# First MoE of a three-stage kernel: gate and value products with the weights as the stationary operand, no transposes of the gated rows

## The chip, the cores and the metric

The kernel runs on one core of a Trainium2 chip. A core has a matrix engine (PE, with its weight loads shown apart as PEld), three elementwise engines (DVE, ACT, POOL), and DMA queues, of which SP issues most here. Each engine works through its own list of instructions in order. The metric is device time in microseconds (us), the median of several executions. The profile is one execution.

## The reference

Three stages follow one another: attention in which every row keeps its 32 largest scores, a gated feed-forward block ("first MoE", one expert), and a routed block of eight experts.

```python
x = topk_attention(q, k, v)                 # 1152 tokens x 512 (8 heads of 64), top 32 of 576 scores
xn = x / rms(x) * rms_g
g = xn @ w_gate                             # 512 -> 1536
silu = g * (1.0 / (1.0 + np.exp(-g)))
val = xn @ w_val                            # 512 -> 1536
y = silu * val @ w_out                      # 1536 -> 512
out = routed_experts(y)                     # 8 experts, each 512 -> 1024 -> 512, one per token
```

The change concerns only `g`, `val` and the way in which `silu * val` reaches the product with `w_out`.

## The kernel before

The 1152 tokens are nine tiles of 128. Attention runs over 36 pairs of heads (nine tiles, four pairs each): scores on PE (L317, tile `tp`), a copy by ACT (L319), the top 32 by DVE (L324 to L379), masking and exponentials by ACT and POOL (L398, L399, L404), nine transposes of the weights by PE (L422, copied by ACT at L423), and the product with the values by PE (L430, tile `xps`).

The first MoE of a tile begins when its four pairs are done. `norm` scales the rows and leaves `xn`, the turned rows (512 channels on partitions, 128 tokens), as a high and a low float16 half. `moe1(t, ew)` then goes over three groups g of 512 hidden channels. For each it computes the gate product and the value product (b = 2g and 2g + 1). A product is 12 matmuls: four chunks c of 128 channels, each with three combinations of high and low halves. `xn` is the stationary operand (a load of 128 x 128) and 512 columns of the weights (`half(i, lo)`, in `wbig`) stream through, so the result `a` in PSUM (tile `pm`, three buffers; `late` for some of the last tile) has tokens on partitions. That is 72 matmuls a tile at L502 and 648 in all.

The gate is activated and multiplied with the value product into `h` (tile `gs`, one buffer; `x` once in the last tile). Tiles 0, 7 and 8 use ACT and DVE for this (L510, L511, L514), tiles 1 to 6 ACT and POOL (L516 to L523, with `gs` also holding the scaled gate, written at L517). The product with `w_out` (L531, 36 matmuls a tile, 128 x 512) needs `h` with the hidden channels on partitions. `turned(g, h)` does that: four 128 x 128 transposes on PE (L486) into a `pm` tile, then `halves`: ACT copies it to the high half of `hT` (L470), DVE subtracts to get the low half (L471). It is called in the middle of the gate product of the next group, and for the last group among the matmuls of L531.

The order on each engine is made by a scheduler from priorities: attention has a head start of 200 to 400 in `ahead`, `moe1` has none, so first-MoE work fills in behind attention and falls behind it. For the last tile (t = 8) the order on PE is fixed by `after(...)`: the products of group g + 1 wait behind the transposes of group g. After the last pair ("the tail") PE has the rest of tiles 6, 7 and 8, while ACT and DVE prepare the first expert weights: squares (L795), high halves (L820, L822), low halves (L825). The routed stage starts at L920 when tile 8 is through.

Of the kernel before, what the change touches and what calls it, by code (L numbers as in the profile page):

```python
# [8 lines left out]
F32 = mybir.dt.float32  # L9
# [53 lines left out]
def whole(  # L63
# [415 lines left out]
    def moe1(t, ew):  # L479
        hT = [mx.tile([P, 2 * KC, P], F16, name="hT", bufs=3) for _ in range(3)]  # L480
        xn = xnT.pop(t)

        def turned(g, h):
            tp = pm.tile([P, 4, P], F32, name="pm")
            for i in range(4):
                behind[t, "turn", g] = nc.tensor.transpose(tp[:, i, :], h[:, i * P:(i + 1) * P], ident)  # L486
            behind[t, "dve"] = halves(hT[g], tp)

        h = None
        for g in range(3):  # L490
            th = mx.tile([P, DM], F32, name="th")
            if ew is nc.gpsimd:
                gs = mx.tile([P, DM], F32, name="gs")
            for w in range(2):
                b = 2 * g + w
                ahead_of = (None, ("prod", 0), None, ("turn", 0), None, ("turn", 1))[b] if t == NT - 1 else None
                a = late[0].tile([P, DM], F32, name="late") if late and b % 3 else pm.tile([P, DM], F32, name="pm")
                for c in range(KC):
                    i = KC * b + c
                    with after(t, *ahead_of) if ahead_of else nullcontext():  # L500
                        for n, (x, lo) in enumerate(((0, 0), (0, 1), (KC, 0))):
                            behind[t, "prod", b] = nc.tensor.matmul(  # L502
                                a, xn[:, x + c, :], half(i, lo), start=(c == 0 and n == 0), stop=(c == KC - 1 and n == 2))
                    if c == 1:
                        yield
                    if c == 0 and w == 0 and h is not None:
                        turned(g - 1, h)
                yield
                if w == 0 and ew is nc.vector:
                    behind[t, "tanh", g] = nc.scalar.activation(th, a, AF.Tanh, scale=gdec[:, g:g + 1])  # L510
                    behind[t, "th", g] = nc.vector.scalar_tensor_tensor(th, th, 1.0, a, op0=OP.add, op1=OP.mult)  # L511
                elif ew is nc.vector:
                    h = mx.tile([P, DM], F32, name="x" if t == NT - 1 and g == 1 else "gs")
                    behind[t, "gs", g] = nc.vector.scalar_tensor_tensor(h, a, vg[:, g:g + 1], th, op0=OP.mult, op1=OP.mult)  # L514
                elif w == 0:
                    nc.scalar.activation(th, a, AF.Tanh, scale=gdec[:, g:g + 1])  # L516
                    nc.scalar.activation(gs, a, AF.Copy, scale=gdec[:, g:g + 1])  # L517
                    ew.tensor_tensor(th, th, gs, op=OP.mult)
                    ew.tensor_tensor(th, th, gs, op=OP.add)
                else:  # L520
                    h = mx.tile([P, DM], F32, name="gs")
                    nc.scalar.activation(h, a, AF.Copy, scale=vdec[:, g:g + 1])
                    ew.tensor_tensor(h, th, h, op=OP.mult)  # L523
        yps = pm.tile([P, DM], F32, name="pm")
        for f in range(NF1):
            i = final(6, f)
            if f == (2 if t == NT - 1 else 4):
                turned(2, h)
            with after(t, *(("prod", 5) if f < 2 else ("turn", 2))) if t == NT - 1 else nullcontext():
                for n, (hi, lo) in enumerate(((0, 0), (0, 1), (1, 0))):  # L530
                    nc.tensor.matmul(yps, hT[f // KC][:, KC * hi + f % KC, :], half(i, lo), start=(f == 0 and n == 0), stop=(f == NF1 - 1 and n == 2))  # L531
            if f % 2 == 1:
# [598 lines left out]
```

## Time and profile before

| what | value |
|---|---|
| median of three runs | 655.77 us (653.97 to 659.06) |
| the profiled execution | 654.35 us, its span 652.4 us |
| granted TensorE clock, mean | 0.984 |
| PE busy | 583.8 us, 89% of the span |
| DVE, ACT, POOL busy | 533.5, 501.6, 355.6 us (82%, 77%, 55%) |
| share of the chain that ended last | PE 61%, DMA 10%, DVE 9%, ACT 8%, POOL 6% |

The span has four parts: loading and weight conversion up to about 147 us, attention together with the first MoE up to 459 us (the last L430), the tail up to 514.4 us (the last transposes of tile 8 before the first L920), and the routed experts to the end. A row of a timeline merges equal instructions that follow one another: its first number is the start, its second the time to the end of the last of them, and x12 says how many. The pace of a run of matmuls is therefore read from ends: the end of one row (start plus duration) minus the end of the row before it, divided by the count. The duration of a single matmul is longer than its pace, because matmuls overlap.

### The profile page before, as it was taken

The numbers are of one execution on the slowest core, as the hardware profiler recorded it, in microseconds if no ns is written. First come the engines' busy times: TensorE is split into PE (matmuls) and PEld (weight loads), VectorE is DVE, ScalarE is ACT, GpSimd is POOL, SyncE is SP. The second block draws the span as 40 slices with busy tenths as digits, with TensorE's granted clock in tenths as the row PEclk, the third lists the DMA queues.
The fourth block names the chain that finished last, engine by engine and source line by source line (L and its number), as shares of the span: only waits on it lengthen the run. The fifth ranks groups of instructions, "written<-read, shape, count | busy, mean of one in ns | idle before, by whom it ended". The sixth has DMA issues, their size and how long they took to land.

```text
span 652.4 us, 13434 instructions
## 1 busy us (share of the span) xinstructions
PE 583.8 (89%) x4817; PEld 409.2 (63%) x4817; DVE 533.5 (82%) x1439; ACT 501.6 (77%) x972; POOL 355.6 (55%) x490
## 2 busy tenths in 40 slices
PE   1427879799999999999999999999999879999995
PEld 1314455445666666767666666565555579999994
DVE  3989999968989979998988999882359756999951
ACT  4469978997787968978887889786499538999811
POOL 2487644646358879958878789686121310123312
PEclk9999979899999999999999999999999989999998
DMA  8998345923000010100000000004900479999201
GB/s 233 296 329 292 118 175 194 311 76 78 30 13 29 14 49 10 34 18 26 18 10 34 16 13 14 2 1 179 354 16 8 156 192 390 340 321 359 97 23 43
DMA packets 47006, 80.05 MB, mean 123 GB/s; under 512 B 18716, under 2 KB 23324, under 8 KB 46930
## 3 DMA queue, kind: packets, MB, share of 16 engines
q1 hardware_dynamic: 45138, 74.28, 35.2%
q0 software_dynamic: 1792, 4.83, 1.9%
q8 instruction: 39, 0.64, 0.4%
q14 instruction: 37, 0.30, 0.1%
HBM read 64.35 MB, written 12.27 MB: 117 GB/s over the span
## 4 chain that ended last, share of the span: by engine, by line
PE 61%; DMA 10%; DVE 9%; ACT 8%; POOL 6%; issue 3%; SPq 2%; POOLq 0%; DVEq 0%; ACTq 0%
PE pm L502 16%; PE acc L920 15%; PE pm L531 9%; PE xps L430 6%; PE tp L317 5%; PE tp L422 4%; ACT junk L795 3%; DMA disp<-wraw 2%; DMA wbig<-in_k_l_dram 2%; DVE r L373 2%; PE pm L486 2%; POOL pp L399 1%; DVE wbig L168 1%; DMA raw<-in_w_dram 1%; DVE wbig L169 1%
## 5 line engine op out<-in xcount | busy, mean ns | idle before, releaser
L502 PE MATMUL pm<-wbig,xn 128*128 128x512 f16 x600 | 145.4, 379 | 0.5 <-DVE hT L471 0.5
L920 PEld LDWEIGHTS <-split 128*128 128x128 f16 x1728 | 114.8, 99 | 5.1 <-DMA xbT<-xb 3.2
L399 POOL TENSOR_TENSOR pp<-s,pp 128x576 f32<-128x576 f32 x72 | 102.1, 1434 | 23.1 <-ACT pp L398 22.9
L502 PEld LDWEIGHTS <-xn 128*128 128x128 f16 x648 | 62.6, 98 | 60.6 <-issue 0.9
L376 DVE MAX8 m<-r 128x8 f32<-128x288 f32 x216 | 96.7, 452 | 2.5
L373 DVE MATCH_REPLACE8 r<-m,r 128x288 f32<-128x288 f32 x216 | 95.2, 443 | 0.0
L317 PE MATMUL tp<-kst,qh 128*128 128x288 f32 (+1 forms) x160 | 64.4, 410 | 32.8 <-ACT s L319 14.9
L531 PE MATMUL pm<-wbig,hT 128*128 128x512 f16 x324 | 76.7, 380 | 0.0
L825 DVE SCALAR_TENSOR_TENSOR split<-raw,sc,split 128x2048 f16<-128x2048 f32 (+1 forms) x32 | 65.9, 2076 | 0.1
L319 ACT ACTIVATE s<-tp 128x288 f32<-128x288 f32 x144 | 57.3, 421 | 10.5 <-PE tp L317 8.8
L423 ACT ACTIVATE pt<-tp 128x384 f32<-128x384 f32 x108 | 52.2, 503 | 15.3 <-PE tp L422 10.8
L317 PEld LDWEIGHTS tp<-kst,qh 128*128 128x128 f32 (+1 forms) x160 | 31.1, 195 | 51.1 <-ACT s L319 21.1
L430 PE MATMUL xps<-pt,vt 128*64 128x128 f32 (+1 forms) x800 | 62.4, 275 | 0.0
L422 PE MATMUL tp<-ident,pp 128*128 128x128 f32 x324 | 57.9, 288 | 4.9 <-DVE r L325 2.6
L398 ACT ACTIVATE pp<-s,bias 128x576 f32<-128x576 f32 x72 | 52.3, 779 | 9.4 <-POOL bias L381 9.3
L920 PE MATMUL acc<-hE,split 128*128 128x168 f16 (+2 forms) x864 | 58.9, 228 | 0.3 <-DVE hE L932 0.3
L404 ACT ACTIVATE pp<-pp,bias 128x576 f32<-128x576 f32 x72 | 57.1, 795 | 2.3 <-POOL pp L399 2.1
L920 PE MATMUL acc<-xgT,split 128*128 128x168 f16 (+1 forms) x768 | 56.4, 234 | 0.4 <-issue 0.4
L795 ACT ACTIVATE junk<-raw 128x2048 bf16<-128x2048 f32 (+1 forms) x32 | 54.1, 1689 | 3.2 <-DMA raw<-in_w_dram 2.9
L422 PEld LDWEIGHTS tp<-ident,pp 128*128 128x128 f32 x324 | 40.2, 145 | 23.7 <-DVE r L325 3.4
L430 PEld LDWEIGHTS xps<-pt,vt 128*64 128x64 f32 x800 | 43.9, 138 | 13.7 <-issue 12.0
L531 PEld LDWEIGHTS <-hT 128*128 128x128 f16 x324 | 29.8, 98 | 32.0 <-issue 1.0
(237 smaller groups left out, 1225.5 us busy)
## 6 DMA issues: line engine op xcount, KB each, us to landing
raw<-in_w_dram SPq DMA_DIRECT2D x28, 1024.0 KB, 9.4
wbig<-in_w_gate_dram SPq DMA_DIRECT2D x6, 1024.0 KB, 7.7
wbig<-in_w_val_dram SPq DMA_DIRECT2D x6, 1024.0 KB, 9.1
wraw<-in_w_out_dram SPq DMA_DIRECT2D x12, 512.0 KB, 5.9
disp<-wraw SPq DMA_DIRECT2D x18, 257.0 KB, 6.4
qraw<-in_q_l_dram SPq DMA_DIRECT2D x72, 64.0 KB, 2.2
wbig<-in_k_l_dram SPq DMA_DIRECT2D x16, 288.0 KB, 4.0
split<-in_w_dram SPq DMA_DIRECT2D x4, 1024.0 KB, 8.3
```

The costliest lines, as they stand in the source:

```text
L317: nc.tensor.matmul(sp[:c1], x[:, i, :c1], kst[b, hp][:, i, c * HALF:(c + 1) * HALF], start=(n == 0), stop=(n == 1))
L319: nc.scalar.activation(s[:, c * HALF:(c + 1) * HALF], sp, AF.Copy)
L373: nc.vector.match_replace(h[i], to[n - 1][:, i], h[i], -3.0e38)
L376: nc.vector.max(to[n][:, i], h[i])
L399: nc.gpsimd.tensor_tensor(w, s[i], w, op=OP.subtract)
L422: nc.tensor.transpose(tp[:, i, :], p2[:, o:o + P], ident)
L430: nc.tensor.matmul(xps[t][rows, hp, c0:c1], v, w, start=(n == 0), stop=(n == 4))
L502: behind[t, "prod", b] = nc.tensor.matmul(a, xn[:, x + c, :], half(i, lo), start=(c == 0 and n == 0), stop=(c == KC - 1 and n == 2))
L531: nc.tensor.matmul(yps, hT[f // KC][:, KC * hi + f % KC, :], half(i, lo), start=(f == 0 and n == 0), stop=(f == NF1 - 1 and n == 2))
L795: nc.scalar.activation(junk, raw[:, g * 2 * BIG // k:(g + 1) * 2 * BIG // k], AF.Square, accum_out=sc[:, 3 + g:4 + g])
L825: nc.vector.scalar_tensor_tensor(lo[:, r], raw[:, r], sc[:, 1:2], hi[:, r], op0=OP.mult, op1=OP.subtract)
L920: nc.tensor.matmul(a, u[:, c, col * P:(col + 1) * P], v[:, c, :a.shape[-1]], start=(c == 0 and n == 0), stop=(c == nk - 1 and n == 2))
```

## The change

Both products are computed turned: 128 columns of the weights are the stationary operand and the 128 tokens of `xn` stream through. A result `a` has the same size and the same place, but now has hidden channels on partitions, as four blocks j of 128 channels, each accumulated over 12 matmuls. A product is thus 48 matmuls of 128 x 128, each with a weight load of its own; a tile has 288 and all nine have 2592. `h` comes out as L531 needs it, so the transposes go, and `halves` reads `h` in SBUF directly (`activated`). The two orders by `after` in the last tile are adapted. What activates and multiplies is unchanged. (In the changed file the product is L499, the product with `w_out` L529, the gate copies L514 and L515.)

```diff
-        def turned(g, h):
-            tp = pm.tile([P, 4, P], F32, name="pm")
-            for i in range(4):
-                behind[t, "turn", g] = nc.tensor.transpose(tp[:, i, :], h[:, i * P:(i + 1) * P], ident)
-            behind[t, "dve"] = halves(hT[g], tp)
+        def activated(g, h):
+            behind[t, "dve"] = halves(hT[g], h.rearrange("p (j w) -> p j w", j=KC))
...
-                ahead_of = (None, ("prod", 0), None, ("turn", 0), None, ("turn", 1))[b] if t == NT - 1 else None
+                ahead_of = ("prod", b - 1) if t == NT - 1 and b else None
...
-                for c in range(KC):
-                    i = KC * b + c
+                for j in range(KC):
                     with after(t, *ahead_of) if ahead_of else nullcontext():
-                        for n, (x, lo) in enumerate(((0, 0), (0, 1), (KC, 0))):
-                            behind[t, "prod", b] = nc.tensor.matmul(
-                                a, xn[:, x + c, :], half(i, lo), start=(c == 0 and n == 0), stop=(c == KC - 1 and n == 2))
-                    if c == 1:
+                        for c in range(KC):
+                            for n, (x, lo) in enumerate(((0, 0), (0, 1), (KC, 0))):
+                                behind[t, "prod", b] = nc.tensor.matmul(
+                                    a[:, j * P:(j + 1) * P], half(KC * b + c, lo)[:, j * P:(j + 1) * P], xn[:, x + c, :],
+                                    start=(c == 0 and n == 0), stop=(c == KC - 1 and n == 2))
+                    if j == 1:
                         yield
-                    if c == 0 and w == 0 and h is not None:
-                        turned(g - 1, h)
+                    if j == 0 and w == 0 and h is not None:
+                        activated(g - 1, h)
...
-                turned(2, h)
-            with after(t, *(("prod", 5) if f < 2 else ("turn", 2))) if t == NT - 1 else nullcontext():
+                activated(2, h)
+            with after(t, "prod", 5) if t == NT - 1 else nullcontext():
```

The scheduler orders the instructions anew, on every engine. Three places are shown, first as they stood and then as they stand.

On PE, in the middle of attention: before, the transposes of `h` (L486, written to `pm`) stand between the matmuls of the product (L502, `xn` loaded).

```order
L447 MATMUL px<-ident,xu 128x128 x4
L486 MATMUL pm<-ident,gs 128x128 x2
L502 LDWEIGHTS xn
L502 MATMUL pm<-wbig,xn 128x512
L502 LDWEIGHTS xn
L502 MATMUL pm<-wbig,xn 128x512
L486 MATMUL pm<-ident,gs 128x128
L502 LDWEIGHTS xn
L502 MATMUL pm<-wbig,xn 128x512
L486 MATMUL pm<-ident,gs 128x128
```

On PE at a like place after: the product is L499, with `wbig` loaded and `xn` streaming, and it stands behind the transposes of the attention weights (L422).

```order
L529 LDWEIGHTS hT
L529 MATMUL pm<-wbig,hT 128x512
L422 MATMUL tp<-ident,pp 128x128 x3
L499 LDWEIGHTS wbig
L499 MATMUL pm<-xn,wbig 128x128
L499 LDWEIGHTS wbig
L499 MATMUL pm<-xn,wbig 128x128
```

The transposes of `h` are gone from the product; where one load of `xn` stood before a matmul of 512 columns, four loads of `wbig` stand before four matmuls of 128.

On PE, at the end of the tail: before, matmuls of L531 on `hT` of tile 8, then the small matmuls of the routing of tile 7 (L598, L599), then the transposes of the last `h` (L486), then the 30 remaining matmuls of L531.

```order
L531 MATMUL pm<-wbig,hT 128x512
L805 LDWEIGHTS ones_70
L805 MATMUL st<-sc,ones_70 128x1
L598 LDWEIGHTS before
L598 MATMUL px<-oh,before 128x8
L599 LDWEIGHTS ones_70
L599 MATMUL px<-cum,ones_70 128x8
L486 MATMUL pm<-ident,gs 128x128 x4
L531 LDWEIGHTS hT
L531 MATMUL pm<-wbig,hT 128x512
```

The same place on PE after (L529 is the product with `w_out`, L596 and L597 are the routing of tile 7).

```order
L529 LDWEIGHTS hT
L529 MATMUL pm<-wbig,hT 128x512
L596 LDWEIGHTS before
L596 MATMUL px<-oh,before 128x8
L597 LDWEIGHTS ones_70
L597 MATMUL px<-cum,ones_70 128x8
L529 LDWEIGHTS hT
L529 MATMUL pm<-wbig,hT 128x512
```

The 36 matmuls of this product (now L529) run on, with only the routing matmuls between them (now L596, L597); nothing on PE stands between them that reads `h` itself.

On ACT, in the middle of attention (the name in brackets is the engine whose counter is waited for): before, the copy of the scaled gate into `gs` (L517) waits for PE, whose transposes were the last readers of the buffer, and the copy `hT` (L470) comes behind it.

```order
L398 ACTIVATE pp<-s,bias 128x576
L423 ACTIVATE pt<-tp 128x384 [waits PE_49,Activation_49]
L517 ACTIVATE gs<-pm,st 128x512 [waits PE_49]
L470 ACTIVATE hT<-pm 128x512
L423 ACTIVATE pt<-tp 128x384 [waits PE_49]
```

On ACT at a like place after (L514 is the tanh of the gate, L584 belongs to the routing).

```order
L470 ACTIVATE hT<-gs 128x512 [waits Pool_49]
L584 ACTIVATE ex,nm<-lg,nm 128x8 [waits Pool_49]
L514 ACTIVATE th<-pm,st 128x512 [waits PE_49]
L515 ACTIVATE gs<-pm,st 128x512 [waits DVE_49]
L398 ACTIVATE pp<-s,bias 128x576 [waits Pool_49]
```

Now `hT` (L470) is copied from `gs` itself, and the next gate copy into `gs` (L515) waits for DVE, whose subtraction (L471) is now the last reader of the one buffer. All 18 gate copies of tiles 1 to 6 wait for DVE in this way.

## Rows read from the trace of the kernel before

**Rows 1.** Windows: attention with first MoE, the tail, its ACT-heavy part

```profile
core 0: us, PE busy (x) PEld busy (x) DVE busy (x) ACT busy (x) POOL busy (x), PEclk, DMA share, GB/s
147.00:459.00 312.00, 310.26 (x2173) 199.72 (x2171) 268.35 (x886) 253.97 (x568) 234.12 (x323) 1.00 0.10 33
459.00:514.40 55.40, 53.68 (x293) 28.39 (x293) 36.53 (x75) 41.73 (x75) 12.52 (x26) 1.00 0.34 122
475.00:507.00 32.00, 31.06 (x179) 16.56 (x178) 26.32 (x54) 30.71 (x55) 5.68 (x11) 1.00 0.08 28
```

**Rows 2.** Longest waits of PE from 147 to 507 us (total, times, longest)

```profile
PE pm L486 <- DVE nm L604: 0.6, 1, 0.6
```

**Rows 3.** Groups by line (busy us, mean ns): weight loads of full arrays

```profile
L920 PEld LDWEIGHTS <-split 128*128 128x128 f16 x1728 | 114.8, 99 | 5.1 <-DMA xbT<-xb 3.2 <-issue 1.5
```

**Rows 4.** Timeline of PE: transposes of h, and 512-column matmuls

```profile
454.12 0.59 PE L531 MATMUL pm<-wbig,hT 128*128 128x512 f16 x2
454.56 0.60 PE L486 MATMUL pm<-ident,gs 128*128 128x128 f32 x4
...
506.46 0.66 PE L486 MATMUL pm<-ident,gs 128*128 128x128 f32 x4 [0.64 <-DVE nm L604]
506.95 6.64 PE L531 MATMUL pm<-wbig,hT 128*128 128x512 f16 x30
```

**Rows 5.** Timeline of PE: float16 matmuls with a new weight load each

```profile
518.54 4.18 PE L920 MATMUL acc<-xgT,split 128*128 128x128 f16 x72
...
524.28 4.79 PE L920 MATMUL acc<-hE,split 128*128 128x128 f16 x83 [0.29 <-DVE hE L932]
532.06 3.84 PE L920 MATMUL acc<-xbT,split 128*128 128x48 f16 x96 [2.98 <-DMA xbT<-xb]
535.74 0.64 PE L961 MATMUL back<-ident,yT 128*128 128x128 f32 x4
```

**Rows 6.** Timeline of PE: borders between kinds of matmul

```profile
74.75 1.08 PE L193 MATMUL tp<-wbig 128*128 128x128 bf16 x16
75.64 0.38 PE L317 MATMUL tp<-kst,qh 128*128 128x288 f32 x1
...
308.23 0.88 PE L430 MATMUL xps<-pt,vt 128*64 128x128 f32 x12
309.03 0.87 PE L422 MATMUL tp<-ident,pp 128*128 128x128 f32 x6
...
337.41 1.25 PE L502 MATMUL pm<-wbig,xn 128*128 128x512 f16 x5
338.31 0.49 PE L317 MATMUL tp<-kst,qh 128*128 128x288 f32 x1
...
338.86 0.88 PE L430 MATMUL xps<-pt,vt 128*64 128x128 f32 x12
339.66 0.40 PE L317 MATMUL tp<-kst,qh 128*128 128x288 f32 x1
```

**Rows 7.** Timeline of ACT and DVE: hT copies and the subtractions behind them

```profile
250.43 0.61 ACT L470 ACTIVATE hT<-pm 128x512 f16<-128x512 f32 x1
...
253.11 0.68 DVE L471 TENSOR_TENSOR hT<-pm,hT 128x512 f16<-128x512 f32 x1
...
353.85 0.60 ACT L470 ACTIVATE hT<-pm 128x512 f16<-128x512 f32 x1
...
355.09 0.67 DVE L471 TENSOR_TENSOR hT<-pm,hT 128x512 f16<-128x512 f32 x1
```

**Rows 8.** Timelines of PE and ACT: marks of the tail

```profile
457.68 1.31 PE L430 MATMUL xps<-pt,vt 128*64 128x128 f32 x20
...
466.06 0.27 PE L544 MATMUL px<-ident,yx 128*128 128x128 f32 x1
...
472.95 0.63 ACT L455 ACTIVATE x<-xu 128x512 f32<-128x512 f32 x1 [0.20 <-DVE xu L452]
...
508.86 0.57 ACT L470 ACTIVATE hT<-pm 128x512 f16<-128x512 f32 x1
```

## The prediction

> **What bounds the kernel now.** I read the windows by stage first, then the waits of PE, then the timeline of PE row by row. The products that change run from 147 us to the end of the tail at 514.4 us. In the attention stretch PE is busy 310.3 of 312 us, in the tail 53.7 of 55.4; DVE has 268.4 of the 312, ACT 254.0, POOL 234.1, and the granted clock is 1.00 throughout [rows 1], which is the 2.4 GHz level. Busy time of PE alone proves little, since matmuls overlap, so the waits count: the longest of PE in these 360 us is 0.64 us [rows 2], and the ends of the rows in its timeline follow one another at a fixed pace. So PE sets the end of both stretches; what its list loses in time the kernel gains, until DVE (86% of the attention stretch) or ACT takes its place. In the tail ACT is the second: 30.7 of 32 us busy from 475 to 507 [rows 1], from the square of tile 8 (ACT L455, 472.95 us) to its last hT copy (508.86 us) [rows 8]. The routed stage hangs on the end of tile 8 and should move with it.
>
> **The change part by part.**
>
> *Transposes removed.* Four of them stand in one row: its end is 455.16, that of the row before 454.71, so 0.45 us for four [rows 4]. 27 groups of four go: 27 x 0.45 = 12.1 us less on PE.
>
> *Products.* Thirty matmuls of 512 columns end 6.47 us after the row before them (513.59 less 507.12), so 0.2157 us each [rows 4]; 648 of them are 139.8 us. For 128 columns with a load each, two runs of L920 are of the very form that the change uses (float16, full array, a new load for each, 12 matmuls into the same 128 columns of PSUM in the first): 72 take 4.18 us and 83 take 4.79, so 11 more take 0.61, 0.0555 us each [rows 5]. 2592 x 0.0555 = 143.9 us: 4.1 us more. A load lasts 99 ns by itself [rows 3], but a pace of 0.0555 shows that it runs under the matmuls before it; with 48 columns, 96 pairs take 3.84 us, 0.040 each [rows 5], so at 128 columns the load is not yet what limits. The upper bound of the pace is 4.18 / 72 = 0.0581, or 10.8 us more.
>
> *Borders.* A 512-column matmul hides the load of whatever follows; one of 128 hides less. A score matmul (L317) ends 0.14 us after a 512-column row, 0.19 after the 128-column rows of L193 (bf16, a load each) [rows 6]: 0.05 us more. Four float32 transposes behind L920 need 0.48 instead of 0.45 [rows 5, 4]: 0.03 more. By the order of PE, products now stand directly before scores 64 times and before float32 transposes and their like 86 times: 3.2 + 2.6 = 5.8 us. Against that, products now separate work that stood together: L430 before scores 10 times instead of 21, where the border is 0.32 instead of 0.14, and before L422 17 times instead of 31, where six transposes need 0.79 instead of 0.675 [rows 6]: 11 x 0.18 + 14 x 0.115 = 3.6 us less. Net 2.2 us more. Bounds: nothing at the new borders (5.8 less than taken), or what a border behind L430 costs at all of them (64 x 0.18 + 86 x 0.115 = 21.4, or 15.6 more). I take the values behind L193 and L920, which use the full array as the new matmuls do; L430 uses 64 columns of it.
>
> *The gap at the end.* Before the last transposes PE stands idle for 0.64 us, waiting for DVE [rows 4]. After, 24 matmuls of the last product (24 x 0.2157 = 5.2 us) cover the making of the last hT: 0.6 us less.
>
> PE in sum: -12.1 + 4.1 + 2.2 - 0.6 = -6.4 us. It does not fall evenly. The new order leaves 576 small matmuls and 96 of L529 behind the last L430, where 132 and 84 and 24 transposes stood: 52.7 us instead of 49.3. So the tail is 3.4 - 0.6 = 2.8 us longer, and the attention stretch some 9.2 us shorter. The work that ACT does in the tail begins earlier with it.
>
> *What is moved and waits.* ACT now copies hT from `gs`, which saves the way through PSUM but keeps the one `gs` buffer until DVE has subtracted; the next gate copy (18 of them) stands on ACT behind that, and behind it the score copies and exponentials that DVE and PE want. DVE ended its subtraction 2.75 us after the ACT copy in one place (253.79 less 251.04) and 1.31 in another (355.76 less 354.45) [rows 7]. In the new order of ACT, 9 of the 18 have only 0.7 to 2.5 us of other work between copy and gate copy, 14.8 us together by the mean durations; the others have more than 2.75. So ACT waits 1.5 us in all at a lag of 1.31 and 9 x 2.75 - 14.8 = 10 us at 2.75. ACT has 58 us free in this stretch [rows 1], so most of it is absorbed: I take 2 us, between 0 and 10. SP and the DMAs change in nothing but their start; the `pm` buffers have three tiles fewer to hold per tile of tokens.
>
> Total: -6.4 + 2 = -4.4 us, 649.95 against the profiled execution's 654.35. The median of the runs, 655.77, lies 1.4 above that execution, so on the median's scale 651.4; I predict 651.
>
> **The rivals.** *The load is not hidden* (slower by far). If each load of 99 ns [rows 3] set the pace, 2592 would take 256.6 us: 116.8 more, less 12.1, about 759. Rows 5 speak against it at the same form. The Trainium skill (TensorE: Matmul & The Clock Gate, "The mechanism" under packing small matmuls) states that a weight load overlaps with matmuls in flight only when it is for other rows of the array; and its section "Back-to-back issue gap" gives a sustained 81 ns per matmul at 128 columns and 131 at 512, by which the products alone would cost 210 - 85 = 125 us more. The trace disagrees with both here: full-array loads run under full-array matmuls, and the paces are 55.5 and 215.7 ns. Chance 0.02.
>
> *Another engine takes the slack* (no change). If DVE, ACT and POOL need the 312 us whatever PE does, only the tail moves: 654.35 + 2.8 = 657, or 658.5 on the median's scale; with half of the 9.2 us kept, 654. For it: DVE would have to work at 268 of 303 us, 89%, with ACT at 84%, and the three feed one another for each pair of heads. Against it: PE hardly waits for them now. Chance 0.22 for 654 to 659.
>
> *ACT waits for DVE at `gs` and PE feels it* (slower). The place is the gate copy of tiles 1 to 6. With the whole 10 us on the path the sum is -6.4 + 10 = +3.6, some 659; if all 18 copies lose 2.75 us it is 49.5 - 6.4, near 699. It decides where the 18 cost over 6.4 us of PE's time, 0.36 us each. For it: such a wait holds up all that stands behind it on ACT. Against it: half of the 18 have room. Chance 0.13, mostly 658 to 668.
>
> *No loss anywhere.* Borders cost nothing and ACT absorbs everything: -12.1 + 4.1 - 3.6 - 0.6 = -12.2, 642 (643.5 on the median's scale). Chance 0.13 for 641 to 646.5.
>
> **How the numbers follow.** The forecast, 646.5 to 654, has 0.50. About 1%, 6.5 us, is what a measurement of this kernel can tell from no change: below 649.2 is faster, above 662.3 slower. Below 649.2 lie the last rival and a bit under half of the forecast: 0.13 + 0.23 = 0.36. Above 662.3 lie the unhidden load and most of the wait at `gs`: 0.02 + 0.09 = 0.11; I give 0.14, since a new order on every engine can hold a wait that I did not see. Within 1%: 0.50. The range 643 to 661 leaves out the unhidden load, the worse part of the wait at `gs` and the best of the last rival, about 2 in 10.
>
> **What would show it.** Right: L499 at 0.0555 us in runs; no L486; the last L430 near 450 us and the first L918 near 509; PE still without waits of over a microsecond; 0.19 us for a score behind L499. The wait at `gs` shows as idle time of ACT before L515 ended by DVE L471; another bound shows as PE idle before L422 or L317, ended by ACT or POOL. The prediction is wrong if L499 runs at 80 ns or more, or if the attention stretch does not shrink.

## The result and the profile after

The changed kernel takes 660.83 us (median of 9 runs, 659.37 to 663.26) beside 654.98 for the kernel before (9 runs, 653.13 to 659.06): a ratio of 1.0078, 95% interval 1.0057 to 1.0098. It is slower by 5.9 us. 651.0 was predicted, 4.8 below before; the range of 643 to 661 holds the time at its very edge, and the direction was wrong.

The profiled execution of after has a span of 658.0 us. That of before (652.4) began its first product at 146.66 us, after at 148.56. Up to there the instructions of both are the same, so I took a second profile of the unchanged kernel before (the run "before again" below): span 653.5, first product at 148.57. With equal starts the two spans differ by 4.5 us, and the windows say where. They are cut at four marks: first product, end of the last L430, end of the last matmul with `w_out`, first copy of the first expert's hidden rows (`hE`) on ACT, end. Windows of after (columns as in rows 1):

```profile
148.56:450.52 301.96, 297.84 (x3575) 246.50 (x3573) 259.62 (x884) 251.00 (x566) 235.03 (x320) 1.00 0.10 32
450.52:513.44 62.92, 59.91 (x729) 47.61 (x728) 39.23 (x75) 44.63 (x77) 17.56 (x26) 0.97 0.34 126
513.44:527.73 14.29, 7.55 (x68) 7.07 (x68) 7.46 (x28) 6.80 (x11) 4.03 (x8) 0.65 0.27 85
527.73:658.00 130.27, 119.92 (x1769) 117.85 (x1767) 96.45 (x125) 86.27 (x96) 25.02 (x17) 0.98 0.71 219
```

The same windows of the kernel before, second profile:

```profile
148.57:460.85 312.28, 310.61 (x2175) 199.92 (x2173) 268.78 (x887) 254.05 (x570) 234.19 (x324) 1.00 0.11 33
460.85:515.46 54.61, 53.67 (x293) 28.37 (x292) 35.74 (x74) 40.98 (x73) 12.55 (x26) 1.00 0.33 122
515.46:523.16 7.70, 5.91 (x66) 5.56 (x67) 6.89 (x27) 4.90 (x9) 1.17 (x3) 0.83 0.55 160
523.16:653.50 130.34, 119.57 (x1770) 118.05 (x1768) 96.98 (x127) 87.66 (x98) 28.28 (x18) 0.98 0.70 221
```

Attention is 10.3 us shorter, the tail 8.3 longer, the way from the end of the tail to the first `hE` 6.6 longer (14.29 against 7.70), the experts equal: -10.3 + 8.3 + 6.6 - 0.1 = +4.5. Beside the first profile of before, the third window is 7.4 longer (14.29 against 6.92) and the experts 1.6 shorter, +3.7 in all. In the third window PE of after is busy for half of the time, at a mean granted clock of 0.65.

**The third window.** PE of after, where rows 4 and 5 stood for before:

```profile
505.46 5.34 PE L529 MATMUL pm<-wbig,hT 128*128 128x512 f16 x24
510.64 0.17 PE L596 MATMUL px<-oh,before 128*128 128x8 bf16 x1
510.69 2.75 PE L529 MATMUL pm<-wbig,hT 128*128 128x512 f16 x12
515.11 0.63 PE L542 MATMUL px<-ident,yx 128*128 128x128 f32 x4 [1.67 <-DVE yn L563]
522.41 7.77 PE L918 MATMUL acc<-xgT,split 128*128 128x128 f16 x89 [1.63 <-DMA xgT<-disp]
```

Tile 7's routing (L596) stands behind 24 of tile 8's matmuls with `w_out`; before, it ran at 505.63, ahead of 30 of them. What hangs on it is seen on DVE, POOL and SP of after:

```profile
507.79 2.48 DVE L823 SCALAR_TENSOR_TENSOR split<-raw,sc,split 128x1024 f16<-128x1024 f32 x2
510.18 2.31 DVE L820 TENSOR_SCALAR split<-raw,sc 128x1024 f16<-128x1024 f32 x2
512.41 2.47 DVE L823 SCALAR_TENSOR_TENSOR split<-raw,sc,split 128x1024 f16<-128x1024 f32 x2
514.80 0.15 DVE L604 SCALAR_TENSOR_TENSOR scr<-px,oh 128x8 f32<-128x8 f32 x1
...
516.11 1.12 POOL L619 DMA_INDIRECT disp<-yd,slot  x1 [0.33 <-POOL slot L617]
...
450.60 60.05 SPq L777 DMA_DIRECT2D raw<-in_w_dram  x6
519.10 1.36 SPq L834 DMA_TRANSPOSE xgT<-disp  x1
```

The masked sum of tile 7's routing (L604) now stands behind six conversions of expert weights on DVE. So the scatter of tile 7's rows (POOL L619) starts at 516.11, the gather of the first expert's rows (SP L834) at 519.10, and the first expert's products wait for it until 522.41. PE's wait of 1.67 us for DVE (L563) ends behind the same six conversions. In the first profile of before the same steps, and PE's first products of the first expert, are:

```profile
505.63 0.17 PE L598 MATMUL px<-oh,before 128*128 128x8 bf16 x1 [0.30 <-POOL oh L595]
514.94 1.51 PE L920 MATMUL acc<-xgT,split 128*128 128x128 f16 x24
...
506.45 0.15 DVE L606 SCALAR_TENSOR_TENSOR scr<-px,oh 128x8 f32<-128x8 f32 x1
...
508.71 1.10 POOL L621 DMA_INDIRECT disp<-yd,slot  x1 [0.29 <-POOL slot L619]
...
511.66 1.36 SPq L836 DMA_TRANSPOSE xgT<-disp  x1
...
513.75 0.37 SPq L779 DMA_DIRECT2D raw<-in_w_dram  x1
```

There the gather was under way before the tail ended, and 24 products of the first expert ran at 514.94, under tile 8's dispatch. On SP the last piece of a weight load stood behind the gather (L779, 513.75); now all six pieces stand ahead of it.

**The second window.** ACT, then PE of after, between 482 and 488 us, and the windows there:

```profile
482.69 0.58 ACT L470 ACTIVATE xn<-xps 128x512 f16<-128x512 f32 x1
...
482.33 0.18 PE L803 MATMUL st<-sc,ones 128*128 128x1 bf16 x1 [0.88 <-DVE sc L806]
482.83 0.16 PE L803 MATMUL st<-sc,ones 128*128 128x1 bf16 x1 [0.32 <-ACT junk L793]
483.31 0.27 PE L499 MATMUL pm<-xn,wbig 128*128 128x128 f16 x2 [0.32 <-ACT xn L470]
484.04 4.13 PE L499 MATMUL pm<-xn,wbig 128*128 128x128 f16 x46 [0.45 <-DVE xn L471]
...
484.00:488.20 4.20, 4.16 (x50) 4.16 (x50) 4.20 (x6) 4.20 (x7) 0.00 (x0) 0.64 0.00 0
488.20:495.00 6.80, 6.80 (x114) 6.33 (x112) 6.80 (x8) 6.71 (x12) 0.00 (x0) 1.00 0.01 2
```

Before, that copy stood here:

```profile
478.36 0.59 ACT L470 ACTIVATE xn<-xps 128x512 f16<-128x512 f32 x1
```

Tile 8's copy of its normed rows on ACT (`xn`) runs at 482.69, behind ten squares of expert weights (L793); before, at 478.36 behind three. PE waits 0.88 + 0.32 us at the sums of these squares (L803), then 0.32 + 0.45 us for the copy and its low half, all in a row, and its next 46 matmuls take 4.13 us instead of the 2.6 that 46 x 0.0556 gives: the clock is 0.64 in their window, 1.00 behind it.

### The profile page after: what moved, and what is told of

Its sections match the earlier page's. It is cut to its first block, busy times and chain, and to the rows that moved or that the text cites. A ratio compares the mean times of both kernels' runs of the same rounds, so it can differ in the third digit from the quotient of the medians.

```text
span 658.0 us, 17080 instructions
## 1 busy us (share of the span) xinstructions
PE 581.0 (88%) x6653; PEld 477.7 (73%) x6653; DVE 529.6 (80%) x1439; ACT 502.3 (76%) x972; POOL 361.0 (55%) x490
## 4 chain that ended last, share of the span: by engine, by line
PE 36%; DVE 22%; POOL 13%; DMA 12%; ACT 8%; issue 5%; SPq 2%; POOLq 0%; DVEq 0%; ACTq 0%
PE acc L918 12%; PE pm L499 10%; DVE r L373 4%; PE pm L529 4%; DVE m L376 3%; DVE split L823 3%; PE xps L430 3%; DMA vt<-in_v_l_dram 3%; POOL pp L399 3%; PE tp L317 2%; DMA raw<-in_w_dram 2%; PE tp L422 2%; DVE wbig L168 2%; DMA disp<-wraw 2%; DVE wbig L169 2%
## 5 line engine op out<-in xcount | busy, mean ns | idle before, releaser
L499 PE MATMUL pm<-xn,wbig 128*128 128x128 f16 x2400 | 167.8, 220 | 2.4 <-DVE th L509 0.9
L499 PEld LDWEIGHTS <-wbig 128*128 128x128 f16 x2592 | 156.5, 99 | 17.1 <-issue 6.0
L918 PEld LDWEIGHTS <-split 128*128 128x128 f16 x1728 | 116.0, 99 | 7.9 <-issue 6.1
L376 DVE MAX8 m<-r 128x8 f32<-128x288 f32 x216 | 95.1, 450 | 1.6
L317 PE MATMUL tp<-kst,qh 128*128 128x288 f32 (+1 forms) x160 | 62.9, 399 | 34.0 <-ACT s L319 16.0
L529 PE MATMUL pm<-wbig,hT 128*128 128x512 f16 x324 | 78.2, 379 | 1.9 <-ACT hT L470 0.9
L398 ACT ACTIVATE pp<-s,bias 128x576 f32<-128x576 f32 x72 | 52.5, 783 | 14.3 <-POOL bias L381 14.2
L422 PE MATMUL tp<-ident,pp 128*128 128x128 f32 x324 | 58.0, 287 | 3.9 <-DVE r L325 2.2
L918 PE MATMUL acc<-xgT,split 128*128 128x168 f16 (+1 forms) x768 | 58.9, 240 | 2.7 <-DMA xgT<-disp 1.6
L793 ACT ACTIVATE junk<-raw 128x2048 bf16<-128x2048 f32 (+1 forms) x32 | 54.2, 1694 | 8.7 <-DMA raw<-in_w_dram 8.2
L918 PE MATMUL acc<-hE,split 128*128 128x168 f16 (+2 forms) x864 | 59.3, 228 | 0.5 <-DVE hE L930 0.5
L423 ACT ACTIVATE pt<-tp 128x384 f32<-128x384 f32 x108 | 50.1, 499 | 12.2 <-PE xps L430 6.9
L430 PE MATMUL xps<-pt,vt 128*64 128x128 f32 (+1 forms) x800 | 57.9, 273 | 0.0
L529 PEld LDWEIGHTS <-hT 128*128 128x128 f16 x324 | 29.3, 98 | 31.4 <-DVE hT L471 1.5
L430 PEld LDWEIGHTS xps<-pt,vt 128*64 128x64 f32 x800 | 43.4, 139 | 10.0 <-issue 7.8
L317 PE MATMUL tp<-kst,ql 128*128 128x288 f32 (+1 forms) x160 | 48.7, 309 | 0.0
```

The costliest lines, as they stand in the source:

```text
L317: nc.tensor.matmul(sp[:c1], x[:, i, :c1], kst[b, hp][:, i, c * HALF:(c + 1) * HALF], start=(n == 0), stop=(n == 1))
L376: nc.vector.max(to[n][:, i], h[i])
L422: nc.tensor.transpose(tp[:, i, :], p2[:, o:o + P], ident)
L430: nc.tensor.matmul(xps[t][rows, hp, c0:c1], v, w, start=(n == 0), stop=(n == 4))
L499: behind[t, "prod", b] = nc.tensor.matmul(a[:, j * P:(j + 1) * P], half(KC * b + c, lo)[:, j * P:(j + 1) * P], xn[:, x + c, :], start=(c = ...
L918: nc.tensor.matmul(a, u[:, c, col * P:(col + 1) * P], v[:, c, :a.shape[-1]], start=(c == 0 and n == 0), stop=(c == nk - 1 and n == 2))
```

## The experiments

The theories at first: (1) the new order behind attention costs, whatever the form; (2) the turned form itself costs; (3) ACT waits for DVE at `gs`; (4) work left over from attention costs behind it. The trace of after settles the third: ACT waited for DVE at L515 for 1.1 us in 3 waits, over 18 gate copies. All runs in one table; stages are cut as above, in us, of the profiled execution (of before, the first); ratios are to the kernel before, run beside each.

| run | time | ratio (95%) | first product at | attention | tail | to first hE | rest |
|---|---|---|---|---|---|---|---|
| before | 654.98 | 1 | 146.7 | 312.3 | 54.6 | 6.9 | 131.9 |
| after | 660.83 | 1.0078 (1.0057, 1.0098) | 148.6 | 302.0 | 62.9 | 14.3 | 130.3 |
| e1 | 661.24 | 1.0077 (1.0045, 1.0109) | 150.3 | 301.9 | 61.2 | 12.4 | 133.6 |
| e2 | 668.60 | 1.0210 (1.0167, 1.0252) | 148.6 | 311.1 | 60.0 | 13.0 | 133.6 |
| e3 | 664.13 | 1.0127 (1.0092, 1.0162) | 149.2 | 302.0 | 63.3 | 11.0 | 136.9 |
| e4 | 661.45 | 1.0071 (1.0047, 1.0094) | 147.8 | 302.0 | 60.8 | 11.7 | 135.7 |
| e5 | 666.93 | 1.0158 (1.0104, 1.0212) | 147.4 | 312.3 | 54.7 | 15.4 | 135.1 |
| e9 | 667.56 | 1.0181 (1.0133, 1.0229) | 146.7 | 312.2 | 54.7 | 14.2 | 135.7 |
| e6 | 665.78 | 1.0129 (1.0066, 1.0192) | 150.7 | 301.8 | 61.1 | 14.1 | 137.5 |
| e7 | 658.26 | 1.0035 (1.0009, 1.0060) | 149.2 | 301.9 | 61.1 | 13.3 | 132.3 |
| e8 | 660.70 | 1.0074 (1.0042, 1.0106) | 148.1 | 301.9 | 64.2 | 10.3 | 133.2 |
| e10 | 657.28 | 1.0022 (0.9992, 1.0052) | 149.3 | 301.9 | 62.4 | 7.5 | 132.3 |
| e11 | 654.54 | 0.9977 (0.9953, 1.0002) | 152.2 | 301.3 | 61.1 | 10.1 | 130.9 |
| e12 = before again | 655.37 (one run) | | 148.6 | 312.3 | 54.6 | 7.7 | 130.3 |
| e13 | 654.80 | 0.9970 (0.9952, 0.9989) | 146.6 | 302.0 | 60.1 | 10.7 | 130.2 |
| e14 | 654.84 | 0.9977 (0.9959, 0.9995) | 148.2 | 301.8 | 61.4 | 9.4 | 131.3 |
| e15 (old form) | 657.65 | 1.0024 (0.9997, 1.0050) | 149.8 | 312.3 | 55.0 | 6.6 | 134.5 |

### Halves of the change: e1 and e2

```diff
+        form = t < NT - 2      # e1; e2: t >= NT - 2; the old form and its transposes otherwise
```

> The turned form for tiles 0 to 6 alone; tiles 7 and 8 keep the form and the waits of before, so that the stretch behind attention is put in order nearly as before (tile 7's routing matmuls stand ahead of most of tile 8's w_out product, and the first expert's 24 matmuls behind tile 8's dispatch transposes). Theory 1 (the loss is the order behind attention, not the form): the 10 us that the attention stretch gained stay and the 14 us lost behind it do not come: 643 to 650 us beside 655 for the kernel before. Theory 2 (the form itself costs, through its four times as many matmuls, in proportion to the tiles): 655 + 7/9 of 5.8 = 659 to 660. Theory 3 (ACT's tanh and the single gs buffer wait for the high and low copies) would show in all tiles that use DVE for the product with the gate, that is tile 0 and 7 and 8: most of its loss goes here as by theory 1. Theory 4 (first-MoE work is left over from the attention stretch and has to be done behind it, whatever the order): the stretch behind attention stays about 8 us longer, so 655 to 658.

> The other half: the turned form for tiles 7 and 8 alone. The order that the scheduler makes at the end is that of the changed kernel (tile 7's two routing matmuls behind 24 matmuls of tile 8's w_out product, 108 matmuls of the first expert behind tile 8's dispatch). Theory 1: no gain in the attention stretch, the loss behind it in full: 655 plus 6 to 14, so 661 to 669 us. Theory 2: 655 + 2/9 of 5.8 = 656 to 657. Theory 4: no more work is left over behind attention than before, so 655 to 657.

e2 came out as theory 1 had it: little gained in attention (1.2 us), the loss behind it in full. e1 did not: 661.2 where 643 to 650 were expected. The order on PE is nearly that of before, tile 7's routing runs at 505.4, and still PE waits 3.86 us for the first expert's rows, where before it waited for none. POOL and SP of e1 show why:

```profile
508.42 1.45 POOL L630 TENSOR_SCALAR slot<-pos 128x1 int32<-128x1 f32 x1
510.16 1.97 POOL L632 DMA_INDIRECT disp<-yd,slot  x1 [0.29 <-POOL slot L630]
...
511.00 0.37 SPq L790 DMA_DIRECT2D raw<-in_w_dram  x1
517.06 1.36 SPq L847 DMA_TRANSPOSE xgT<-disp  x1
```

The slot and the scatter run while DVE converts weights (508.51 to 510.98): 1.45 and 1.97 us where before, with DVE idle, they took 0.38 and 1.10. A megabyte of weights is issued ahead of the gather, which then starts 4.9 us behind the end of the scatter's instruction, 1.9 before. How much of this is the load's is not shown here: in after a load stands ahead of the gather too, and the gather starts 1.9 us behind. So theory 1 had to be read more widely: not the order on PE alone, but when tile 7's rows reach memory, through PE, DVE, POOL and SP.

### Two places of the order mended: e3 and e4

```diff
-            with after(t, "prod", 5) if t == NT - 1 else nullcontext():
+            with after(t - (f > 1), *(("prod", 5) if f < 2 else ("pe",))) if t == NT - 1 else nullcontext():
...   (e4 also)
     with after(NT - 1, "sq"):
         size(0, 0)
+    with after(NT - 1, "xn high"):
         size(1, 1)
```

> The changed kernel with one wait more: matmuls 3 to 12 of w_out's product in tile 8 are issued behind tile 7's last routing matmul. The order then has tile 7's routing 18 matmuls earlier on PE, its masked sum ahead of three conversions on DVE, and 24 of the first expert's matmuls ahead of tile 8's routing. Tile 8's copy of the normed rows is still behind ten squares on ACT. Theory 1: the 5.8 us lost between the end of w_out's product and the end come back, those lost ahead of it stay: 660.8 - 5.8 = 655, 652 to 657 us. Theory 2 (the form) and theory 4 (work left over): no change, 659 to 662.

> As the run before, and the second group of squares of the expert weights is issued behind tile 8's copy of the normed rows, so that four squares stand ahead of that copy on ACT and not ten (as in the kernel before). Theory 1: of the 8.3 us that the stretch behind attention lost, the 3 to 4 us of stalls on the squares and the slower matmuls behind them come back too: 648 to 654 us, faster than both kernels. Theory 2 and theory 4: no change, 659 to 662.

e3 was slower than the changed kernel, not faster: PE waits 1.55 us for GpSimd's `oh` (which expert each row takes) at tile 7's routing, the scatter still starts only at 513.77 us and takes 1.81, and the rest is 6.6 us longer, where PE waits 4.5 us for DVE's part of `hE` (1.6 in after) and 2.6 for a square (1.6 in after). e4 gave 2.1 us of the tail back (62.9 to 60.8), as the copy in front of the squares should, but no time: now `yx` is late.

```profile
510.83 2.19 ACT L818 ACTIVATE split<-raw,sc 128x1024 f16<-128x1024 f32 x2 [3.80 <-DVE sc L807]
...
513.65 1.12 PE L542 MATMUL px<-ident,yx 128*128 128x128 f32 x4 [3.02 <-ACT yx L533]
```

Two conversions (L818) stand on ACT ahead of the copy of tile 8's product, and wait for a scale that DVE works out behind two conversions of its own. PE idles 3.02 us instead of 0.78. Two places mended were not enough; the stretch has a chain over five engines, and each place mended showed the next.

### The same order in the kernel before: e5 and e9

```diff
+        while t == NT - 2 and (NT - 1, "out", 7) not in behind:
+            yield
+        with after(NT - 1, "out", 7) if t == NT - 2 else nullcontext():
             nc.tensor.matmul(lp[:, 1, :], before, oh, start=True, stop=False)
```

("out", 7 is the last of the first 24 matmuls with `w_out`. In e9 tile 8's counts also wait for tile 7's; in e5 they were taken without them, so rows were written to other places.)

> The kernel before, with its form of the products and its transposes, and one wait more: tile 7's two routing matmuls are issued behind 24 of the 36 matmuls of w_out's product in tile 8, where they stand in the changed kernel. The order of the rest follows: tile 7's masked sum goes behind three conversions on DVE, the second half of the fifth expert load goes ahead of the gather of the first expert's rows on SP's queue, and 108 matmuls of the first expert stand behind tile 8's routing. Theory 1 (the order costs, whatever the form): the first expert starts 6 to 8 us later and the time is 5 to 8 us longer, 660 to 664 beside 655 to 656. Theory 2 (the form costs): no change, 654 to 658. This run also gives a second profile of a kernel with the order of before up to the first product, whose start (146.7 us before, 147.8 to 150.3 in the five others) has no cause in the change.

> The kernel before once more with tile 7's two routing matmuls behind 24 matmuls of tile 8's w_out product, and with tile 8's counts taken behind tile 7's, as in the kernel before (in the run of this edit above they were taken without them, so that rows were written to other places). The order of every engine is that of the run above. Theory 1: the 10 us of that run again, 663 to 668. If they came from the other places: 655 to 658.

This is the plainest pair of runs of the study. With not one matmul of the new form, another place for two matmuls of 8 columns, with what the scheduler then moves behind them on DVE, PE and SP, costs 12 us (1.0181 in e9). Attention and tail are those of before to 0.1 us; the way to the first `hE` is 14.2 us as in after, and the rest is longer too. PE and POOL of e9:

```profile
510.76 0.17 PE L603 MATMUL px<-oh,before 128*128 128x8 bf16 x1
516.41 1.09 PE L544 MATMUL px<-ident,yx 128*128 128x128 f32 x4 [2.84 <-DVE yn L565]
523.61 4.59 PE L925 MATMUL acc<-xgT,split 128*128 128x128 f16 x56 [2.17 <-DMA xgT<-disp]
...
517.42 1.12 POOL L626 DMA_INDIRECT disp<-yd,slot  x1 [0.35 <-POOL slot L624]
```

The marks are those of after: scatter at 517.42, first product of the first expert at 523.61. Theory 1 is shown for this stretch. I had put the price at 5 to 8 us; it was more, since the rest grew by another 4: there PE waits 3.7 us for one square on ACT, where it waited 0.4 us in two waits before.

### Further places, one after the other: e6, e7, e8

```diff
+            with tc.issue_after(xg["a"].ins) if n == 4 and g == 1 else nullcontext():   # e6: on top of e4
                 nc.sync.dma_start(dst[:, g * m:(g + 1) * m], src[:, g * m:(g + 1) * m])
...
-    with after(NT - 1, "dve"), after(NT - 1, "tanh", 2):
+    with after(NT - 1, "dve"), after(NT - 1, "yx"):                # e7: on top of e6
         convert(3, 3, True, (0, 1))
...
+    with after(NT - 2, "yh"):                                      # e8: on top of e7
         size(3, 3)
```

> The changed kernel with the routing and the copy first, as in the run of that name (661.5 us), and the second half of the fifth expert load issued behind the gather of the first expert's rows on SP's queue, where it stands in the kernel before. The order of the expert products becomes that of before as a result. Theory 5 (this megabyte's transfer stands in the way of tile 7's scatter and of the gather): the scatter lands 1 to 3 us earlier, and the time is 657 to 660. If the load is no obstacle: 660 to 663.

> As the run before, and ACT's two conversions of the fourth expert matrix are issued behind its copy of tile 8's w_out product (yx), for which PE waited 3.0 us in the run with routing and copy first and 0.8 in the kernel before. Theory 1: another 2 us less, 654 to 658. Otherwise the time of the run before.

> As the run before, and the four squares of the fourth expert matrix are issued behind ACT's copy of tile 7's rows in 16 bits, for which tile 7's scatter waited 2 us on POOL (rows ready at 508.3, slots at 506.2). Theory 1: tile 7's scatter starts 1 to 2 us earlier and the first expert with it: 652 to 657. If the squares' own result is then late (it is needed for the conversions): 656 to 660.

e6 put the load behind the gather, and the gather came 2.0 us behind the scatter's instruction instead of 2.7 in e4: 0.7 us, less than the 1 to 3 expected. It lost far more elsewhere:

```profile
518.49 2.65 PE L920 MATMUL acc<-xgT,split 128*128 128x128 f16 x24 [1.28 <-DMA xgT<-disp]
520.93 1.82 PE L556 MATMUL px<-rg,xu 128*128 128x8 f32 x8
```

As in the kernel before, 24 products of the first expert now stand ahead of tile 8's router product (L556). There the rows had come in time and the products filled a gap; here they had not, and the router of tile 8, with all that hangs on it, stood behind the wait. e7 took the wait for `yx` back to 0.78 us and 7.5 us of the time, more than the 2 expected, and not by that place alone (the rest is 5 us shorter). e8 brought the first `hE` 3 us nearer, but its tail grew by 3.1 us: PE waited 0.85 us for a square that had been put back and 1.32 at tile 7's routing, and the 10 matmuls with `w_out` behind that took 4.00 us, 0.4 each instead of 0.2157, at a granted clock of 0.57. It came near the second outcome that was written down for it.

### All places at once, and the form by itself: e10, e11, e13, e14, e15

On top of e6, e11 makes these edits (e10 the same, with `ev` on DVE for tile 7 too; e13 and e14 are e11 and e10 with tile 7's routing behind 12 matmuls of tile 8 instead of 6):

```diff
-    with after(NT - 1, "dve"):
+    size(3, 3)
+    with after(NT - 1, "dve"), after(3, "bk"):       # "bk": the fourth matrix has its scale
         convert(2, 2, False, (2, 3))
     fetch_w()
-    size(3, 3)
...
-        if t == NT - 1:
+        if t >= NT - 2:                              # tile 7's 16-bit rows as tile 8's
             nc.scalar.activation(yh, y, AF.Copy, scale=yn[:, 5:6])
...
-                with nullcontext() if early is None or c < early else after(NT - 1, "pe"):
+                with nullcontext() if early is None else after(NT - 1, "r0" if c < early else "pe"):
...
-    with after(NT - 1, "slot"), after(NT - 1, "gate"):
+    with after(NT - 1, "slot"), after(NT - 1, "gate"), after(NT - 1, "yl"):
         convert(3, 3, False, (2, 3))
...
-            with after(NT - 1, "act"):
+            with after(NT - 1, "act"), after(NT - 1, "yh"):
                 size(ORDER[4], 4)
```

> The changed kernel with the order of the stretch behind attention mended at each place seen so far: tile 7's routing ahead of 30 of tile 8's 36 w_out matmuls, the second matrix's squares behind tile 8's copy, the second half of the fifth load behind the first gather, the scale of the fourth matrix ahead of the last two conversions of the third on DVE, tile 7's places and slots on DVE instead of GpSimd, tile 7's 16-bit rows by one copy on ACT and one difference on DVE as in tile 8, the first expert's first 24 matmuls behind tile 8's router product, the fifth matrix's squares and the last conversions behind tile 8's 16-bit rows. Theory 1: tile 7's scatter starts at 506 to 508 on the clock of the kernel before (516.1 in the changed kernel), the first expert's first group ends within 7 to 9 us of the end of w_out's product (14.3 in the changed kernel, 6.9 before), and the time is 650 to 656. If the form itself or the work left over cost what was lost, it stays at 658 to 662.

> As the run before, but tile 7's places and slots stay on GpSimd, whose instructions run beside DVE's conversions. In the runs so far a slot took 0.38 us and a scatter 1.1 us where DVE was idle, and 1.2 to 1.5 and 1.8 to 2.0 us beside conversions. Theory 1: tile 7's scatter starts 1 to 2 us later than in the run before and the time is 0 to 2 us longer, 651 to 658.

> The kernel before, unchanged, for a second profile: its first product started at 146.7 us in the first one, and at 147.4 to 150.7 in nine runs whose instructions are the same up to there. If that is scatter, it starts anywhere from 147 to 151 here; if the form of the products moves it, at 146 to 147.5.

These edits were worth 6 us: e11 at 0.9977 beside after at 1.0078, without a change to the form of the products. All but one of them change only the order; tile 7's 16-bit rows are also made by other instructions. Moving the slots to DVE did not pay: the scatter then took 1.09 us, but PE waited 1.20 us at tile 7's routing for places that DVE made behind a conversion. The intervals of e10 and e11 overlap, and e14 and e13, the same pair with a later routing, do not differ. e12 shows that the later start of after (148.6 for 146.7) is scatter.

> As the run with the edits without slots on DVE (654.5 us, 0.998 of the kernel before), but tile 7's routing matmuls stand behind 12 matmuls of tile 8's w_out product instead of 6, so that PE does not wait 0.5 us there for the places. Theory 1: 0 to 1 us less, 652 to 656. If the routing is then late for the first gather: 655 to 658.

> As the run with the nine edits (657.3 us; PE waited 1.2 us for the places at tile 7's routing and 0.7 us for squares), with tile 7's routing matmuls behind 12 matmuls of tile 8's w_out product instead of 6. Theory 1: both waits go, 1 to 2 us less, 653 to 657.

> The kernel before, in the form of before for all tiles, with the edits of the run with the edits without slots on DVE. Its difference from that run is what the form of the products is worth once the order behind attention is alike. Theory 1 with the 4.5 us that the form gained up to the end of w_out's product in every run of it with a mended copy: 3 to 5 us above that run, 656 to 660. If the form's gain does not reach the end (given back in the expert stage, by transfers or by the order there): the same as that run, 653 to 656.

e13 beats both kernels, by little: 0.9970 of the kernel before (0.9952 to 0.9989), and about 7 us under the changed one by the two ratios (1.0078 - 0.9970 = 0.0108). e15, the old form with the edits of e11, stands at 1.0024, so with the same edits the form is worth 0.0054 of 655, 3.5 us, against e13, and 0.0047, 3.1 us, against e11, whose routing edit it has. By the intervals either figure can be off by 2 us or a little more. That is within the 3 to 5 of theory 1. Theory 2 has fallen: the form gains. The edits brought the old form nothing (1.0024), so against the best kernel of the old form, before itself, the gain of e13 is 0.0030, 2 us. In e13 attention and tail together are 362.1 us, 4.8 less than the 366.9 of before; 3 to 4 of these are given back where the first gather is still late:

```profile
506.85 1.95 POOL L619 DMA_INDIRECT disp<-yd,slot  x1 [0.29 <-POOL slot L617]
...
514.48 2.72 PE L920 MATMUL acc<-xgT,split 128*128 128x128 f16 x24 [2.54 <-DMA xgT<-disp]
```

The end of the tail came forward by 5 us, to 508.76, but tile 7's scatter by 2, since its chain over ACT, DVE and POOL did not get shorter. PE's gain ends at that chain.

## Why the prediction was wrong

**Right: what the new matmuls cost.** Two runs of L499 in attention:

```profile
340.34 2.84 PE L499 MATMUL pm<-xn,wbig 128*128 128x128 f16 x48
...
346.50 3.34 PE L499 MATMUL pm<-xn,wbig 128*128 128x128 f16 x57
```

Nine more matmuls take 0.50 us, 0.0556 each; 0.0555 was taken from L920. The border from L499 to a score matmul is 0.19 us at the median of 64, as taken. So the rival of the load that is not hidden is out, and so is the one in which borders cost nothing.

**Right, and a little too careful: attention with the wait at `gs`.** -9.2 and +2 predicted, -10.3 measured. PE stays the engine that sets the stretch, so the rival in which another engine takes the slack is out. PE is without work for 4.1 us there instead of 1.7 (302.0 less 297.8 busy, 312.3 less 310.6), but its longest wait is 0.9 us, once, on an hT copy, and ACT waited at `gs` for 1.1 us in all: most of the 2 us was not needed, and that rival is out.

**Mis-sized: the tail, +2.8 predicted, +8.3 measured.** The work left over was counted rightly: 576 small matmuls and 96 of L529 do stand there. But I said that ACT's work in the tail begins earlier with PE's, and priced the order on ACT, the second engine of that stretch by my own reading, at nothing. Tile 8's copy went behind ten squares instead of three. PE is without work for 3.0 us of the tail instead of 0.9 (62.92 less 59.91, 54.61 less 53.67), and the clock that fell behind its waits cost 4.13 - 2.6 = 1.5 us more; together 3.6 of the 5.5. e4, with the copy ahead of the squares, got 2.1 us back. Of the other 1.9 us, 0.4 are four more transposes of rows (L465: eight in the tail, 0.87 us, instead of four, 0.49); the rest I have not separated.

**Failed: "the routed stage hangs on the end of tile 8 and should move with it."** It hangs on the end of tile 7 as well, through its routing, masked sum, slots, scatter and the first gather, and by an estimate that chain had next to nothing to spare. In after, where PE waited for it, the gather took 3.3 us (519.10 to 522.41); with as much before, issued at 511.66, it was ready at about 514.97, and the first products ran at 514.94. I had said that the first L918 would run near 509; it ran at 522.41. The change of place of tile 7's routing was in front of me: the rows of the new order that stand under the change show L596 and L597 among the matmuls of the last product, where they had stood ahead of the last transposes. I read there what had gone (the transposes), not what had moved, and gave tile 7's routing a term in neither stretch. The sentence that SP and the DMAs "change in nothing but their start" failed with it, since a load went ahead of the gather. The price: 6.6 us from the end of the tail to the first `hE`, where the prediction had nothing. e9 shows the mechanism in the old form by itself (7.3 us there, and 4 in the rest).

**The sum.** -9.2 + 2.8 + 2 = -4.4 predicted, on the profiled execution; -10.3 + 8.3 + 6.6 - 0.1 = +4.5 measured at equal starts. The tail's 5.5 and the third window's 6.6 are the miss; attention and the wait at `gs` gave 3.1 the other way. That 660.83 still lies within 643 to 661 is luck: the upper end was set by the wait at `gs`, which did not come.

**The chances.** A new order that holds a wait I did not see had 0.03 (0.14 for slower, less the 0.11 of the named cases). The change let a scheduler order five engines anew around waits that were set by hand for the old form, and the variants of this study came out in other orders; 0.03 was far too small. By the prediction's own 1% the result (0.9% slower) counts as no change, which had 0.50; but that rested on the slow half of the forecast and on another engine taking the slack, and neither came.

## What to carry to other kernels

A shorter stretch on the engine that sets the pace gains only if the next stage's inputs come earlier too: follow the chain that feeds that stage backwards over every engine and queue, and note how much it has to spare before crediting the gain. Where a scheduler makes the order, compare the place of each instruction that ends such a chain, however small, before and after; here the place of two matmuls of 8 columns, with what moved behind it, cost 12 us, as much as the prediction credited for 108 transposes. Waits that were written by hand for one form of the work have to be set again for another.

## What the hardware showed that I had not expected

**GpSimd beside DVE's conversions.** An operation on 128x1 elements took 0.27 us on POOL with DVE idle (before, L610) and 2.30 beside a conversion (after):

```profile
508.01 2.30 POOL L608 TENSOR_SCALAR yd<-nm,yn 128x1 f32<-128x1 f32 x1
510.39 1.55 POOL L576 TENSOR_TENSOR yd<-yx,yd 128x512 f16<-128x512 f32 x1
```

Spans on POOL are rough, but the next instruction starts as late. DVE is held up too: in e3 a conversion that began together with GpSimd's subtraction took 2.25 us, the one before it 1.28.

```profile
509.81 2.25 DVE L823 SCALAR_TENSOR_TENSOR split<-raw,sc,split 128x1024 f16<-128x1024 f32 x1
...
509.82 1.15 POOL L576 TENSOR_TENSOR yd<-yx,yd 128x512 f16<-128x512 f32 x1
```

The scatters tell the same: 1.10 to 1.12 us with DVE idle for all or most of it, 1.78 to 1.97 for tile 7's beside conversions (e1, e3, e4, e13). How much is lost may hang on when the scatter begins: tile 8's took only 1.26 to 1.27 beside two conversions (before, e4, e13), where it began some 0.3 us before the end of the first (taken as 1.28 us long); tile 7's in e3 and e13 began 0.8 and 1.0 us before it. The Trainium skill ("SBUF — State Buffer", "SBUF: two separate sides") states that DVE and GpSimd share a pair of ports as an exclusive lock, which the one that starts first keeps for its whole instruction (DVE in a 2-port mode or with two inputs in SBUF), and that a DMA issued by GpSimd cannot have its descriptors written while DVE is in a 2-port mode. The trace agrees with the first in the times above, and with the second in so far as scatters beside conversions are longer; no run here separated the lock from other causes or shows DVE's mode.

**The clock after short waits.** Four waits of 1.97 us together within 2.6 us were followed by matmuls at 0.09 us each under a mean granted clock of 0.64, a mix of the levels of 1.2 and 2.4 GHz. In e4, 0.69 and 0.48 us of waits at the same place were followed by 21 matmuls in 1.33 us, at the full level. In the third window of after the clock is 0.65 and the first 89 products of the first expert take 7.77 us; before, 72 took 4.18 [rows 5], 0.058 each. A late gather was thus paid twice here, by the wait and by the matmuls behind it. But such a fall is not the late gather's alone. In the second profile of before PE had the waits of the first (0.78, 0.26 and 0.76 us) and none for the gather, and yet the same 72 took 5.81 us, at a clock of 0.51 from 520.46 to 523.16:

```profile
520.46 5.81 PE L920 MATMUL acc<-xgT,split 128*128 128x128 f16 x72
```
